# Attention units issued in a written order on every engine, with the identity and bias tables built on VectorE

## The chip, the core and the metric

The program runs on one core of a Trainium2 chip. The metric is the device time of one execution in microseconds (us). The kernel before took 1388.05 us, the median of three runs from 1387.29 to 1388.94.

## What is computed

Three layers, each fed by the one before. The sizes: 2 batches, 8 heads, 768 positions, 64 elements a head; then 1536 tokens of 512 elements, 8 experts of 512 to 1024 to 512.

```python
def _attn_ref(q, k, v, n_global, n_local):
    scores = scale * np.matmul(q, k.transpose(0, 1, 3, 2))
    rel = pos[:, None] - pos[None, :]
    is_global = pos[None, :] < int(n_global)
    is_local = (rel >= 0) & (rel < int(n_local))
    keep = is_global | is_local
    dist = np.where(is_global & ~is_local, float(n_local), np.abs(rel))
    scores = scores - slopes[:, None, None] * dist[None, :, :]
    scores = np.where(keep, scores, -1000000000.0)
    a = np.exp(scores - np.max(scores, axis=-1, keepdims=True))
    a = a / (np.sum(a, axis=-1, keepdims=True) + 1e-09)
    return np.matmul(a, v)

def _moe_ref(x, w_gate, w1, w2):
    P = np.exp(x @ w_gate - (x @ w_gate).max())
    for _ in range(8):
        P /= P.sum(1, keepdims=True) + 1e-09
        P /= P.sum(0, keepdims=True) + 1e-09
        P *= N / E
    for e in range(E):
        h = np.maximum(x @ w1[e], 0.0)
        out += P[:, e:e + 1] * (h @ w2[e])
    return out
```

The third layer has the same sizes with gate and weights of its own. Each token goes to one expert there, in the order of falling logits, up to 192 tokens an expert. With 8 global keys and 96 local ones, a query of the attention sees few keys.

## The kernel before

Products are made in three parts of 16 bits: a high half and the rest of each operand, high by high, high by low and low by high (`mm3`, lines 664 to 666). A matrix is first read for its largest magnitude (the tile wam, line 607 on VectorE), brought to a power of two, and split: high half on ScalarE (line 618), low half on VectorE (line 619).

The attention goes through 12 blocks of 128 queries, each in two **units** of four heads: 24 units t = 0 to 23, block t // 2. A block sees 232 keys (128 of its own, 96 before them, 8 global ones), the first block of each batch (units 0, 1, 12 and 13) only 128. The steps of a unit are functions of `band_attention`:

- `start`: q and k of a block are turned by TensorE through the identity (tiles pq and pk, lines 440 and 445), q copied by ScalarE (442) and k by VectorE (slab, 447). GpSimd adds the 104 other keys to the slab (450 to 453).
- `weigh`: TensorE makes the scores (ps, 465); VectorE adds the bias table of a head and takes the extreme (one custom instruction for a head, 471, here called the **softening**); ScalarE takes the exponential (474); VectorE makes the reciprocal of the sum (476, 477) and GpSimd multiplies by it (481, the **normalisation**).
- `turn`: TensorE turns the weights (pe, 491), ScalarE and VectorE copy them out (et, 496 and 494).
- `mix`: TensorE multiplies them with v (pa, 510).
- `split_x`: a finished block is split into halves (xt, 519 on ScalarE, 520 on VectorE), and multiplied with the gate (pg, lines 138 and 139; small instructions 142 and 145).

From unit 12 on, each unit also takes one of the 16 **early products** of expert 0 (ph, through `hidden`): 12 matmuls of 128x512, evacuated twice by ScalarE (657, 658) and once by VectorE (659). Fifteen of them are issued inside the loop over units. The weights of expert 0 are loaded, measured and split meanwhile by two generators, `early`, a step or two a unit.

The bias tables (`table`) and the identity come from ramps that GpSimd writes (jp, line 87; rel, lines 389 and 392). The narrow table's eight products are VectorE's, the wide one's GpSimd's:

```python
            eng = nc.vector if own_only else nc.gpsimd
            for h in range(H):
                eng.tensor_scalar(tb[:, h, :], rel, 2.0 ** (-8.0 * (h + 1) / H), NEG, op0=ALU.mult, op1=ALU.min)
```

The order in which an engine issues is set by a scheduler from the program's data dependences and its own estimates; the loop over units sets priorities only. Loads go through SP's queue in the order that it chose for SP.

Of the kernel before, what the change touches and what calls it, by code (L numbers as in the profile page):

```python
# [40 lines left out]
def tile_sparse_attention_moe_moe(ctx, tc, q, k, v, ng, nl, wg1, w11, w12, wg2, w21, w22, out, taps=None):  # L41
# [117 lines left out]
    gw1 = load_gate(wg1, "wg1")  # L159

    def attention(atp, aps):

        qtz = []
# [186 lines left out]
    def band_attention(atp, aps):  # L350


        order = [(b, i) for b in range(B) for i in range(NBLK)]
        NB = len(order)
        HU = HP // 2
# [14 lines left out]
        def load(n):  # L370
            if n >= NB:
                return
            qbs[n] = rows(q, n, "qb", 3)
            kbs[n] = rows(k, n, "kb", 3)
            b, i = order[n]
            if i:
# [7 lines left out]
        def table(own_only):  # L384
# [4 lines left out]
            nc.gpsimd.iota(rel[:, 0:P], pattern=[[-1, P]], base=0, channel_multiplier=1,  # L389
                           allow_small_or_imprecise_dtypes=True)  # L390
            if not own_only:
                nc.gpsimd.iota(rel[:, P:wl], pattern=[[-1, NP]], base=NP, channel_multiplier=1,
                               allow_small_or_imprecise_dtypes=True)
            m = atp.tile([P, W], F32, name=f"keep{W}")
# [14 lines left out]
            tabs.append(tb)  # L409

        scales, vams = {}, {}

        def magnitude(n):

            b, i = order[n]
            if i == 0:
                vams[b] = sml.tile([P, NBLK + 1], F32, name="vam")
            nc.vector.tensor_reduce(vams[b][:, i:i + 1], vos[n], axis=AX.XY, op=ALU.max, apply_absolute_value=True)

        def batch_scale(b):  # L420

            am = vams.pop(b)
            nc.vector.tensor_reduce(am[:, NBLK:], am[:, :NBLK], axis=AX.X, op=ALU.max)
            s = pow2_scale(am[:, NBLK:], "sv", bufs=2)
            f = sml.tile([P, 1], F32, name="gf")
            nc.vector.tensor_mul(f, s[:, 1:2], gw1[1][:, 1:2])
# [3 lines left out]
        slabs, kgs = {}, {}  # L430

        def start(n):

            b, i = order[n]
            S = SimpleNamespace(n=n, b=b, i=i, W=WB if i else P, nch=2 if i else 1, ex={}, et={}, pa=None)
            S.cks = [P, NP + ng][:S.nch]
            qb, kb = qbs.pop(n), kbs.pop(n)
            pt = aps.tile([P, HP, P], F32, name="pq", tag="tr", bufs=2)
            for p in range(HP):
                nc.tensor.transpose(pt[:, p, :], qb[:, 2 * p:2 * p + 2, :].rearrange("p h d -> p (h d)"), ident)  # L440
            S.qt = atp.tile([P, HP, P], F32, name="qt", bufs=2)
            nc.scalar.activation(S.qt, pt, AF.Copy, scale=qs)
            pt = aps.tile([P, HP, P], F32, name="pk", tag="tr", bufs=2)
            for p in range(HP):
                nc.tensor.transpose(pt[:, p, :], kb[:, 2 * p:2 * p + 2, :].rearrange("p h d -> p (h d)"), ident)
            S.slab = slabs[n] = atp.tile([P, HP, WB], F32, name="slab", bufs=3)
            nc.vector.tensor_copy(S.slab[:, :, 0:P], pt)
# [3 lines left out]
            else:  # L451
                nc.gpsimd.tensor_copy(S.slab[:, :, P:P + NP], slabs.pop(n - 1)[:, :, P - NP:P])
                nc.gpsimd.tensor_copy(S.slab[:, :, P + NP:], kgs[b])
            S.vs = [vos[n]] + ([vps.pop(n)] if i else [])
            return S

        def weigh(S, u):

            W = S.W
            ex = S.ex[u] = atp.tile([P, 2, 2, WB], F32, name="ex", bufs=3)  # L460
            st = sml.tile([P, 4, 4], F32, name="st4", bufs=4)
            ps = [aps.tile([P, 2, 256], F32, name=f"ps{j}", tag=f"sc{j}", bufs=1) for j in range(2)]
# [5 lines left out]
            for y in range(HU):  # L468
                for j in range(2):
                    z = 2 * y + j  # L470
# [57 lines left out]
        for n in range(1, NBLK + 1):  # L528
            load_own(n)
# [6 lines left out]
        for t in range(len(units) + 3):  # L536
            n, u = divmod(t, 2)
            if u == 0:
                load(n + 2)
                if n:  # L540
                    load_own(n + NBLK)
# [637 lines left out]
```

## Time and profile before

| | |
|---|---|
| median of the runs | 1388.05 us |
| the profiled execution | 1384.17 us |
| its span in the trace | 1382.3 us |
| TensorE busy | 1308.7 us, 95% of the span |
| VectorE busy | 808.3 us, 58% |
| ScalarE busy | 591.8 us, 43% |
| GpSimd busy | 211.3 us, 15% |
| attention, up to the end of the 15th early product | 171.1 us |

In the rows below PE is TensorE's matmuls, PEld its weight loads (they lie beside PE), DVE is VectorE, ACT is ScalarE, POOL is GpSimd. L471 is line 471 of the kernel. A row of a timeline gives the start in us, the duration in us, engine, line, operation, the tile written and the tile read, shape and count; in brackets the idle time of the engine before it and what ended that. Rows of the same kind that follow each other on an engine are drawn together, with their count.

### The profile page before, as it was taken

The numbers are of one execution on the slowest core, as the hardware profiler recorded it, in microseconds if no ns is written. First come the engines' busy times: TensorE is split into PE (matmuls) and PEld (weight loads), VectorE is DVE, ScalarE is ACT, GpSimd is POOL, SyncE is SP. The second block draws the span as 40 slices with busy tenths as digits, with TensorE's granted clock in tenths as the row PEclk, the third lists the DMA queues.
The fourth block names the chain that finished last, engine by engine and source line by source line (L and its number), as shares of the span: only waits on it lengthen the run. The fifth ranks groups of instructions, "written<-read, shape, count | busy, mean of one in ns | idle before, by whom it ended". The sixth has DMA issues, their size and how long they took to land.

```text
span 1382.3 us, 19944 instructions
## 1 busy us (share of the span) xinstructions
PE 1308.7 (95%) x7956; PEld 670.7 (49%) x7956; DVE 808.3 (58%) x1765; ACT 591.8 (43%) x1053; POOL 211.3 (15%) x323
## 2 busy tenths in 40 slices
PE   5899999999999999999899999999999989879998
PEld 3665544444444444444344444445545434337775
DVE  5777686554666466556546655575635898822121
ACT  3667551343243324333522434166553566613332
POOL 5233211010001000000100010000001333430100
PEclk8999999999999999999999999999999999989999
DMA  8352024151545135324424441431001111378640
GB/s 217 82 150 74 1 74 170 61 197 47 173 145 170 61 126 179 122 87 158 149 95 142 143 160 57 169 123 62 2 1 63 62 62 62 122 208 302 273 201 24
DMA packets 88557, 164.93 MB, mean 119 GB/s; under 512 B 50065, under 2 KB 50065, under 8 KB 85905
## 3 DMA queue, kind: packets, MB, share of 16 engines
q1 hardware_dynamic: 77040, 119.62, 26.7%
q0 software_dynamic: 11424, 44.05, 8.3%
q8 instruction: 62, 1.02, 0.3%
q14 instruction: 31, 0.25, 0.1%
HBM read 119.61 MB, written 44.05 MB: 118 GB/s over the span
## 4 chain that ended last, share of the span: by engine, by line
PE 47%; DVE 15%; issue 15%; DMA 13%; ACT 5%; POOL 5%; POOLq 0%; DVEq 0%; ACTq 0%
DMA raw<-in_moe_w_dram 7%; PE ph L664 7%; PE ph L666 7%; PE ph L665 7%; PE py L664 6%; PE py L665 6%; PE py L666 6%; DMA ws<-spill 6%; DVE wam L607 4%; DVE wslot L619 2%; POOL acc L761 2%; PE pe L491 2%; PE pa L510 2%; DVE xt L953 1%; DVE xt L955 1%
## 5 line engine op out<-in xcount | busy, mean ns | idle before, releaser
L664 PE MATMUL py<-wslot,hslot 128*128 128x512 f16 x768 | 291.3, 379 | 9.9 <-ACT relu L658 9.9
L664 PE MATMUL ph<-xt,wslot 128*128 128x512 f16 x768 | 291.4, 379 | 7.4 <-ACT relu L658 3.9
L665 PE MATMUL py<-wslot,hslot 128*128 128x512 f16 x768 | 291.3, 379 | 0.0
L666 PE MATMUL py<-wslot,hslot 128*128 128x512 f16 x768 | 291.3, 379 | 0.0
L666 PE MATMUL ph<-xt,wslot 128*128 128x512 f16 x768 | 291.3, 379 | 0.0
L665 PE MATMUL ph<-xt,wslot 128*128 128x512 f16 x768 | 291.2, 379 | 0.0
L657 ACT ACTIVATE hslot<-ph 128x512 f16<-128x512 f32 x192 | 114.5, 596 | 208.9 <-PE ph L666 208.7
L659 DVE TENSOR_TENSOR hslot<-relu,hslot 128x512 f16<-128x512 f32 x192 | 131.5, 688 | 119.6 <-ACT relu L658 118.6
L607 DVE TENSOR_REDUCE wam<-raw 128x1 f32<-128x1024 f32 (+1 forms) x136 | 152.5, 1149 | 74.6 <-DMA raw<-in_moe_w_dram 74.5
L618 ACT ACTIVATE spill<-raw,s 128x1024 f16<-128x1024 f32 x64 | 72.8, 1146 | 246.4 <-DVE s L114 129.8
L619 DVE SCALAR_TENSOR_TENSOR spill<-raw,s,spill 128x1024 f16<-128x1024 f32 x64 | 81.7, 1284 | 114.4 <-ACT spill L618 113.2
L658 ACT ACTIVATE relu<-ph 128x512 f32<-128x512 f32 (+1 forms) x224 | 130.1, 581 | 0.0
L665 PEld LDWEIGHTS <-hslot 128*128 128x128 f16 x768 | 75.3, 98 | 98.9 <-issue 13.6
L665 PEld LDWEIGHTS <-wslot 128*128 128x128 f16 x768 | 75.1, 98 | 93.8 <-issue 9.5
L664 PEld LDWEIGHTS <-hslot 128*128 128x128 f16 x768 | 75.3, 98 | 88.6 <-issue 2.5
L666 PEld LDWEIGHTS <-hslot 128*128 128x128 f16 x768 | 75.1, 98 | 88.5 <-issue 2.5
L666 PEld LDWEIGHTS <-wslot 128*128 128x128 f16 x768 | 75.1, 98 | 87.4
L664 PEld LDWEIGHTS <-wslot 128*128 128x128 f16 x768 | 75.1, 98 | 87.4 <-issue 2.4
L618 ACT ACTIVATE wslot<-raw,s 128x1024 f16<-128x1024 f32 (+1 forms) x72 | 70.9, 1047 | 72.3 <-PE py L666 48.7
L619 DVE SCALAR_TENSOR_TENSOR wslot<-raw,s,wslot 128x1024 f16<-128x1024 f32 (+1 forms) x72 | 81.2, 1159 | 4.3 <-ACT wslot L618 4.3
L650 POOL DMA_DIRECT2D ws<-spill x64 | 44.2, 692 | 220.8 <-DVE spill L619 220.5
L102 POOL PARTITION_ALL_REDUCE amax<-wam x30 | 10.6, 354 | 413.9 <-DVE wam L608 406.0
(245 smaller groups left out, 1652.6 us busy)
## 6 DMA issues: line engine op xcount, KB each, us to landing
raw<-in_moe_w_dram SPq DMA_DIRECT2D x64, 1024.0 KB, 5.9
ws<-spill POOLq DMA_DIRECT2D x64, 512.0 KB, 6.6
w2slot<-ws SPq DMA_DIRECT2D x16, 2048.0 KB, 10.2
hd<-hslot POOLq DMA_DIRECT2D x2, 2048.0 KB, 7.2
hslot<-hd SPq DMA_DIRECT2D x2, 2048.0 KB
qb<-in_q_dram SPq DMA_DIRECT2D x12, 256.0 KB, 3.4
kb<-in_k_dram SPq DMA_DIRECT2D x12, 256.0 KB, 6.6
vo<-in_v_dram SPq DMA_DIRECT2D x12, 256.0 KB, 3.7
```

What stands on the lines that cost most here:

```text
L491: nc.tensor.transpose(pe[:ck, y, j, :], ex[:, y, j, a * P:a * P + ck], ident)
L510: nc.tensor.matmul(S.pa[64 * j:64 * j + 64, p, :], S.vs[a][:ck, 2 * p + j, :], ets[a][:ck, y, j, :], start=a == 0, stop=a == S.nch - 1, ti ...
L607: nc.vector.tensor_reduce(am[:, y:y + 1], raw, axis=AX.X, op=ALU.max, apply_absolute_value=True)
L618: nc.scalar.activation(hi, raw, AF.Copy, scale=s[:, 0:1])
L619: nc.vector.scalar_tensor_tensor(lo, raw, s[:, 0:1], hi, op0=ALU.mult, op1=ALU.subtract)
L650: nc.gpsimd.dma_start(dr[:, :, a * q4:a * q4 + q4], t)
L657: nc.scalar.activation(hi, ps, AF.Relu, scale=HS)
L658: nc.scalar.activation(r[:, :n], ps, AF.Relu, scale=HS)
L659: nc.vector.tensor_sub(lo, r[:, :n], hi)
L664: nc.tensor.matmul(out_, lhs(0, a), rhs(0, a), start=a == 0, stop=False)
L665: nc.tensor.matmul(out_, lhs(0, a), rhs(1, a), start=False, stop=False)
L666: nc.tensor.matmul(out_, lhs(1, a), rhs(0, a), start=False, stop=a == n - 1)
```

## The change

1. The ramp `colx` is written on VectorE by doubling, turned in squares of 32 to a column `rowx`, and identity, jp and both tables come from these two. GpSimd writes no ramp, and the wide table's eight products are VectorE's.
2. The attention's trace of instructions is fixed in its written order on every engine, SP included, through dependences without a semaphore (`in_order`).
3. The loop over units is written anew for that order: scores, the next block's turned q and k (odd units), mixing of unit t−2, turning of unit t−1, the gate product (even units), the early product. The early product's evacuation stands ahead of the next unit's softenings. The first one follows unit 13 in place of unit 12.
4. The weights of expert 0 (`matrix`) are split into eight parts each: two magnitudes a unit, then two splits a unit; every second low half is a multiplication and a subtraction on GpSimd.
5. ScalarE and VectorE change places in the copies of the turned weights; the gate's weights are scaled in steps inside the loop; loads are issued in another order.

The core of the difference:

```diff
-    jp = cst.tile([P, P], I32)
-    nc.gpsimd.iota(jp, pattern=[[1, P]], base=0, channel_multiplier=-1)
+    colx = cst.tile([P, P], F32)
+    nc.vector.memset(colx[:, 0:1], 0.0)
+    n = 1
+    while n < P:
+        nc.vector.tensor_scalar(colx[:, n:2 * n], colx[:, 0:n], float(n), None, op0=ALU.add)
+        n *= 2
+    jp = cst.tile([P, P], F32)
+    blk = jp[:, 0:32]
+    nc.vector.transpose(blk, colx[:, 0:32])
+    rowx = cst.tile([P, 1], F32)
+    for g in range(P // 32):
+        nc.vector.tensor_scalar(rowx[32 * g:32 * g + 32], blk[32 * g:32 * g + 32, 0:1], 32.0 * g, None, op0=ALU.add)
     ident = cst.tile([P, P], F32)
-    nc.vector.tensor_scalar(ident, jp, 0.0, None, op0=ALU.is_equal)
+    nc.vector.tensor_scalar(ident, colx, rowx, None, op0=ALU.is_equal)
...
+    @contextmanager
+    def in_order():
+        traced = nc.cur_bb.bb.instructions
+        last = traced[-1]
+        yield
+        start = next(k for k in reversed(range(len(traced))) if traced[k] is last) + 1
+        before = {}
+        for i in traced[start:]:
+            if i.engine in before:
+                tc.add_manual_dep(i, before[i.engine].name,
+                                  mybir.DependencyInfo(mybir.DependencyClass.NoSync, mybir.DependencyReason.DATA),
+                                  reason="in_order")
+            before[i.engine] = i
...
-            eng = nc.vector if own_only else nc.gpsimd
             for h in range(H):
-                eng.tensor_scalar(tb[:, h, :], rel, 2.0 ** (-8.0 * (h + 1) / H), NEG, op0=ALU.mult, op1=ALU.min)
+                nc.vector.tensor_scalar(tb[:, h, :], rel, 2.0 ** (-8.0 * (h + 1) / H), NEG, op0=ALU.mult, op1=ALU.min)
...
+                nc.scalar.activation(hi, part, AF.Copy, scale=s[:, 0:1])
+                if a % 2:
+                    nc.gpsimd.tensor_scalar(part, part, s[:, 0:1], 0.0, op0=ALU.mult, op1=ALU.add)
+                    nc.gpsimd.tensor_tensor(lo, part, hi, op=ALU.subtract)
+                else:
+                    nc.vector.scalar_tensor_tensor(lo, part, s[:, 0:1], hi, op0=ALU.mult, op1=ALU.subtract)
...
-        for t in range(len(units) + 3):
+        for t in range(NU + 4):
             n, u = divmod(t, 2)
...
+            if t == 1:
+                next(weights)
+            if S:
+                scores(S, u)
+            block = None
+            if u and n + 1 < NB:
+                block = turn_block(n + 1)
+                next(block)
+            if 0 <= t - 2 < NU:
+                m, x = divmod(t - 2, 2)
+                mix(blocks[m], x)
...
+                last = turn(blocks[m], x)
+                next(last)
+            if evac is not None:
+                finish(evac)
+                evac = None
+            for z in range(4):
+                if S:
+                    soften(S, u, z)
+                if z == 0 and block:
+                    next(block)
+            if block:
+                finish(block)
...
+            for x in running:
+                next(x)
+                next(x)
+            if t == 0:
+                table(False)
...
+            for i in magnitudes.get(t, ()):
+                magnitude(i)
+            if S:
+                normalise(S, u)
+            if last:
+                finish(last)
+            for x in running:
+                finish(x)
+            running = []
...
+            elif t >= 4:
+                for _ in range(2):
+                    if not owing:
+                        owing = next(weights, None) == "bank"
+            if mixed and mixed[0].b in scales:
+                x = split_x(mixed.pop(0))
+                next(x)
+                running.append(x)
+            if first_hidden and (0, 0) in W and all(c in split for c in range(first_hidden[0][1] * CPB,
...
+                evac = first_products(*first_hidden.pop(0))
+                next(evac)
...
-            band_attention(atp, aps)
+            with in_order():
+                band_attention(atp, aps)
```

The listings of the two kernels' orders show what moves. **GpSimd at the start**, before (jp and rel are the ramps, kg the global keys, tab_211 the wide table, ex the weights that are normalised; the ISA of line 87 is the library switch for the ramps):

```order
L87 ISA
L87 IOTA jp 128x128
L389 IOTA rel_154 128x128
L389 IOTA rel_201 128x128
L392 IOTA rel_201 128x96
L450 COPY kg<-slab 128x32
L452 COPY slab<-slab 128x4x96
L453 COPY slab<-kg 128x4x8 x2
L452 COPY slab<-slab 128x4x96
L408 TENSOR_SCALAR tab_211<-rel_201 128x232 x2
L481 TENSOR_SCALAR ex<-ex,st_180 128x128 x4
L408 TENSOR_SCALAR tab_211<-rel_201 128x232 x6
```

and now:

```order
L549 COPY kg<-slab 128x32
L583 ISA
L583 TENSOR_SCALAR ex<-ex,st_187 128x128 x4
L541 COPY slab<-slab 128x4x96
L542 COPY slab<-kg 128x4x8
L583 TENSOR_SCALAR ex<-ex,st_255 128x128 x4
```

The ramps and the wide table have left GpSimd, and its library switch stands behind the copy of the global keys, ahead of the first normalisation.

**TensorE in an even unit with an early product**, before (the end of a product, then the gate product pg):

```order
L666 LDWEIGHTS wslot
L666 MATMUL ph<-xt,wslot 128x512
L138 LDWEIGHTS xt
L138 MATMUL pg<-wg1hl,xt 128x16
L139 LDWEIGHTS xt
L139 MATMUL pg<-wg1hl,xt 128x16
```

and now:

```order
L632 LDWEIGHTS xt
L632 MATMUL pg<-wg1hl,xt 128x16
L634 LDWEIGHTS xt
L634 MATMUL pg<-wg1hl,xt 128x16
L839 LDWEIGHTS wslot
L839 MATMUL ph<-xt,wslot 128x512
```

The gate product has moved from behind the unit's early product to in front of it.

**VectorE in the same unit**, before (from the last softening of a unit to the first of the next):

```order
L471 ISA ex,st_1205<-ps_1207,tab_211 128x232
L471 ISA st_1205 128x1
L607 TENSOR_REDUCE wam_946<-raw 128x1
L608 TENSOR_REDUCE wam_946<-wam_946 128x1
L494 COPY et<-pe 104x512
L476 TENSOR_SCALAR st_1205<-st_1205 128x4
L477 RECIPROCAL st_1205<-st_1205 128x4
L520 SCALAR_TENSOR_TENSOR xt<-pa,sv,xt 128x4x128
L142 TENSOR_SCALAR gt<-pg,gf 128x8
L659 TENSOR_TENSOR hslot<-relu,hslot 128x512
L145 SCALAR_TENSOR_TENSOR logits<-pg,gf,gt 128x8
L471 ISA ex,st_1285<-ps_1286,tab_211 128x232
```

and now:

```order
L569 ISA ex,st_1296<-ps_1265,tab_206 128x232
L569 ISA st_1296 128x1
L626 SCALAR_TENSOR_TENSOR xt<-pa,sv,xt 128x4x128
L578 TENSOR_SCALAR st_1296<-st_1296 128x4
L579 RECIPROCAL st_1296<-st_1296 128x4
L602 COPY et<-pe 128x512
L638 TENSOR_SCALAR gt<-pg,gf 128x8
L639 SCALAR_TENSOR_TENSOR logits<-pg,gf,gt 128x8
L500 TENSOR_REDUCE wam_1080<-raw 128x1 x2
L834 TENSOR_TENSOR hslot<-relu,hslot 128x512
L569 ISA ex,st_1386<-ps_1341,tab_206 128x232
```

The low half of x (xt) stands directly behind the four softenings, which stand behind the subtraction of the early product before.

## Rows read from the trace of the kernel before

**Rows 1.** Windows: stretch, its us, busy PE, PEld, DVE, ACT, POOL, granted clock, DMA share, GB/s.
```profile
0.00:13.00 13.00, 4.22 (x23) 3.47 (x24) 5.80 (x33) 2.68 (x4) 2.22 (x10) 1.00 0.88 196
13.00:83.00 70.00, 57.45 (x430) 39.91 (x430) 51.90 (x199) 42.25 (x131) 33.41 (x71) 0.85 0.53 132
50.00:58.00 8.00, 7.55 (x34) 5.12 (x32) 5.41 (x22) 4.64 (x13) 3.67 (x9) 0.58 0.01 3
83.00:171.00 88.00, 85.79 (x650) 51.24 (x647) 63.21 (x214) 54.97 (x152) 26.96 (x59) 1.00 0.25 72
171.00:280.00 109.00, 109.00 (x507) 49.47 (x506) 76.67 (x161) 38.42 (x55) 11.52 (x20) 1.00 0.30 103
```

**Rows 2.** Timeline of TensorE at the end of the attention.
```profile
168.55 0.38 PE L664 MATMUL ph<-xt,wslot 128*128 128x512 f16 x1
...
171.14 0.27 PE L105 MATMUL bc<-ident,gam 128*128 128x128 f32 x1
```

**Rows 3.** Timeline of the start, all engines.
```profile
6.80 0.69 DVE L418 TENSOR_REDUCE vam<-vo 128x1 f32<-128x512 f32 x1 [3.98 <-DMA vo<-in_v_dram]
...
8.10 0.23 POOL L87 IOTA jp<- 128x128 int32 x1 [7.66 <-issue]
...
8.94 1.06 PE L440 MATMUL pq<-ident,qb 128*128 128x128 f32 x4
...
11.77 1.17 DVE L408 TENSOR_SCALAR tab<-rel 128x128 f32<-128x128 f32 x8
...
12.88 0.29 DVE L471 CUSTOM_DVE_ANT_0 ex<-ps,tab 128x128 f32<-128x128 f32 x1
...
17.57 1.42 POOL L481 TENSOR_SCALAR ex<-ex,st 128x128 f32<-128x128 f32 x4
...
19.08 6.31 POOL L408 TENSOR_SCALAR tab<-rel 128x232 f32<-128x232 f32 x6
...
19.45 1.93 PE L465 MATMUL ps<-slab,qt 64*128 64x232 f32 x8
```

**Rows 4.** What lines 87 and 707 issued: count, ns, first and last start.
```profile
L87 POOLq MODIFY_POOL_CONFIG  x2: 11/11/11, 0.8 to 0.8; - x2
...
L707 POOLq MODIFY_POOL_CONFIG  x2: 11/11/11, 166.4 to 166.5; - x2
L707 POOL PARTITION_ALL_REDUCE gm<-gm x1: 377/377/377, 172.1 to 172.1; - x1
```

**Rows 5.** Timeline of one even unit with an early product.
```profile
141.73 1.05 PE L465 MATMUL ps<-slab,qt 64*128 64x232 f32 x8
...
142.33 0.59 ACT L658 ACTIVATE relu<-ph 128x512 f32<-128x512 f32 x1
...
142.96 0.69 DVE L659 TENSOR_TENSOR hslot<-relu,hslot 128x512 f16<-128x512 f32 x1 [0.27 <-ACT relu L658]
...
143.57 0.39 DVE L471 CUSTOM_DVE_ANT_0 ex<-ps,tab 128x232 f32<-128x232 f32 x1
...
144.78 0.39 PE L664 MATMUL ph<-xt,wslot 128*128 128x512 f16 x1
...
144.85 0.69 DVE L494 COPY et<-pe 104x512 f32<-104x512 f32 x1
```

**Rows 6.** First softenings of units 4 and 12, and the first early product.
```profile
35.16 0.40 DVE L471 CUSTOM_DVE_ANT_0 ex<-ps,tab 128x232 f32<-128x232 f32 x1 [0.19 <-PE ps L465]
...
80.98 0.28 DVE L471 CUSTOM_DVE_ANT_0 ex<-ps,tab 128x128 f32<-128x128 f32 x1
...
83.43 0.39 PE L664 MATMUL ph<-xt,wslot 128*128 128x512 f16 x1
```

**Rows 7.** Groups by form up to 172 us: busy us, mean ns | idle before.
```profile
L619 DVE SCALAR_TENSOR_TENSOR wslot<-raw,s,wslot 128x512 f16<-128x512 f32 x16 | 11.7, 742 | 0.0
```

**Rows 8.** Timeline of GpSimd late in the program, two instructions with two inputs each.
```profile
1196.85 5.75 POOL L761 TENSOR_TENSOR acc<-acc,relu 128x512 f32<-128x512 f32 x1 [5.43 <-ACT relu L760]
1204.01 1.09 POOL L761 TENSOR_TENSOR acc<-acc,relu 128x512 f32<-128x512 f32 x1 [1.41 <-ACT relu L760]
```

More of the change, by code (lines that the diff above doesn't have):

```diff
@@ L368, in load_own, with load_qk, load_past @@
                 vos[n] = rows(v, n, "vo", 8)
[L370 to L376, printed above, removed]
+        def load_qk(n):
+            if n < NB:
+                qbs[n] = rows(q, n, "qb", 3)
+                kbs[n] = rows(k, n, "kb", 3)
+        def load_past(n):
+            if n < NB and order[n][1]:
+                b, i = order[n]
                 t = atp.tile([P, H, D], F32, name="vp", bufs=3)
@@ L434, in start, with matrices, turn_block @@
+        def matrices():
+            for which in range(2):
+                yield from matrix(which)
+        slabs, kgs, blocks = {}, {}, {}
+        def turn_block(n):
             b, i = order[n]
-            S = SimpleNamespace(n=n, b=b, i=i, W=WB if i else P, nch=2 if i else 1, ex={}, et={}, pa=None)
+            S = blocks[n] = SimpleNamespace(n=n, b=b, i=i, W=WB if i else P, nch=2 if i else 1, ex={}, et={}, pa=None,
+                                            st={}, ps={})
             S.cks = [P, NP + ng][:S.nch]
@@ L531, in band_attention @@
         nc.scalar.activation(warm, ones[:, 0:1], AF.Exp)
-        blocks = {0: start(0)}
         table(True)
-        units = [(n, u) for n in range(NB) for u in range(2)]
-        splits = []
-        for t in range(len(units) + 3):
+        finish(turn_block(0))
+        weights = matrices()
+        running = []
+        owing = False
+        evac = None
+        magnitudes = {0: (0,), 1: (1, 2), 2: (3, 4), 3: (5,)}
+        magnitudes.update({t: (t - 3,) for t in range(9, 9 + NBLK)})
+        mixed = []
@@ L537, in band_attention @@
+        scaling = None
+        for t in range(NU + 4):
             n, u = divmod(t, 2)
+            S = blocks.get(n) if t < NU else None
             if u == 0:
[L539 to L547 removed]
@@ L548, in band_attention @@
-            for x in splits:
-                next(x, None)
-            if t < len(units):
-                weigh(blocks[n], u)
+                load_qk(n + 3)
+                load_past(n + 1) if n else None
+                load_own(n + 6)
+            if t == 1:
[9 more added lines that the diff above has]
+                mix(blocks[m], x)
+                if x:
+                    mixed.append(blocks.pop(m))
@@ L552, in band_attention @@
+            if owing:
+                next(weights)
+                owing = False
+            for x in running:
+                next(x)
+                next(x)
             if t == 0:
                 table(False)
[L554 to L563 removed]
@@ L586, in tile_sparse_attention_moe_moe @@
+        for x in running:
+            finish(x)
+        finish(weights)
     pools = {}
@@ L734, in tile_sparse_attention_moe_moe @@
         pools["h", n] = lat
-    for x in first_hidden:
-        hidden(*x)
+    for e, tb, f in first_hidden:
+        hidden(e, tb, [f])
     hidden(0, NTB - 1)
```

235 lines of the change are left out of this document (149 added, 86 removed).

## The prediction

> **What bounds the kernel now.** I read the table of windows first, then the timeline of the start, the timelines of one unit in the middle and of the end of the attention, and last the groups by form.
>
> The windows [rows 1] say which stage a gain can come from. From 171 to 280 us TensorE is busy 109 of 109 us. Its order there is the same in both kernels, so whatever makes the attention end earlier is passed on one for one. The profiled execution took 1384.17 us, 3.9 below the median of 1388.05. I work the sum out as a difference and take it from the median. One part in 500, 2.8 us, is about what a measurement of this kernel can tell from no change.
>
> The attention ends when the 15th early product of expert 0 ends: it starts at 168.55 and the next work stands at 171.14 [rows 2]. Twelve matmuls take 2.59 us.
>
> The start [rows 3]: GpSimd's first own instruction, the ramp jp, comes at 8.10, and behind it the identity, the four transposes of q at 8.94, and the first softening of scores at 12.88. The third load on SP, v of block 0, had landed by 6.80, and q and k stand ahead of it. Thus not the data but GpSimd was late. Why: the line of jp issues a library switch at 0.8 and runs at 8.1, and another switch at 166.4 is followed by its first work at 172.1 [rows 4]. A switch costs 5.7 to 7.3 us.
>
> Between 13 and 83 us TensorE is busy 57 of 70 us, VectorE 52, so hand-overs bind; from 83 to 171 TensorE has 86 of 88 [rows 1].
>
> **The change, part by part.** Times are starts of the first softening of a unit, before and now.
>
> *Start.* The identity now needs some 13 short VectorE instructions. From the 128-wide table's eight products, 1.17 us together [rows 3], 0.15 each, and a transpose of 0.2 to 0.7, they end near 3.7. q and k then bind: below the 6.80 of the load behind them, I take 4.5. Two groups of transposes at 1.06 each [rows 3], a copy of k at 0.69 and scores at 1.0 (sizes of the copy at 144.85 and the scores at 141.73, [rows 5]): first softening at 8.3 instead of 12.88, **4.6 earlier**. Ends: 7.5 if q and k are there with the identity, 10.6 if only with v.
>
> *Units 0 to 3.* GpSimd's library switch isn't gone. It stands in front of the first normalisation now, behind the copy of the global keys at 8.4. At 5.7 to 7.3 us [rows 4], unit 0 is normalised from 14.1 to 15.7 on instead of 17.57. The wide table's eight products leave GpSimd, where six of them took 6.31 us ahead of unit 1's normalisation. On VectorE I price them at 0.27 each, the narrow product scaled by 232/128: 2.1 us, beside the library switch. What is late next is TensorE, which has idled: eight score matmuls took 1.93 us at 19.45 [rows 3] against 1.05 at 141.73 [rows 5]. I put unit 4's softening at 31.0 against 35.16 [rows 6], **4.2 earlier**. Ends: 1.9 earlier, if only the smaller library gain is kept; 6.3 more, 8.2 earlier, if the six products' time is saved whole.
>
> *Units 4 to 12.* Before, 35.16 to 80.98 [rows 6], 5.73 a unit. Now VectorE's written order has per unit: four softenings 1.28 and a copy of the turned weights 0.69 [rows 5], two short ones 0.35; an odd unit the copy of k 0.69, an even one the low half of x 0.74 and two small ones 0.45; and either two magnitudes of W1, 0.69 each as for v in [rows 3], or one low half at 0.74 [rows 7] with the other on GpSimd. That is 4.6 in the mean, with 0.4 of waits 5.05; eight units and 1.1 for W1's scale give 41.5, so unit 12 starts at 72.5 against 80.98, **8.5 earlier**. Ends: 4.7 and 5.73 a unit, 69.7 and 76.8.
>
> *First product.* It stood in unit 12 and now ends unit 13, so one more unit lies ahead of it. With 3.7 us each for units 12 and 13 (128 keys) it starts at 80.0 against 83.43 [rows 6].
>
> *Units with a product.* From an odd unit on, TensorE's order is scores, eight transposes, sixteen mixing matmuls, product: the first three take 3.05 us from 141.73 to the product at 144.78 [rows 5]. An even unit's new order puts the gate product of x ahead of the product, and it waits for VectorE. From the product's end at 141.73: two evacuations on ScalarE end at 142.92, the subtraction leads to softenings at 143.57, the fourth ends at 144.85 [rows 5], that is 3.1 us behind; the low half of x 0.74, the gate product 0.25 and the product 2.59 make 6.7. Without that wait the unit would be 3.05 + 0.2 + 2.59 = 5.8. An odd unit has the transposes of q and k, 1.06 each at the low pace [rows 3], 1.15 both at the ratio 1.05 to 1.93: 3.05 + 1.15 + 2.59 = 6.8, with a hand-over of 0.2 7.0. Nine units, 14 to 22, five even: 61.5. Then the last five products (12.9) with units 22 and 23 turned and mixed (6.8): 19.7. The first product itself takes 2.6. So the 15th ends at 80.0 + 2.6 + 61.5 + 19.7 = 163.8 against 171.14: **7.3 us earlier**.
>
> Edits without a cost of their own: W2's splits in units 19 to 22 lie beside products of 2.59. W1's two loads of 1 MB now stand behind some 4 MB on SP, read by VectorE at the end of unit 4, near 34; at the 196 GB/s of the first 13 us [rows 1] the first half lands near 27, the second at 32. Were they late, every softening behind them on VectorE would be too.
>
> The time is 1388.05 − 7.3 = 1380.8, say **1381**.
>
> *A rule against the change.* On GpSimd an instruction with two inputs took 5.75 us at 1196.85 and 1.09 at 1204.01 [rows 8]; the change gives GpSimd four such subtractions on W1 and four on W2. I take 1.1, since each has a unit's time to end in. The Trainium skill ("SBUF — State Buffer", section "SBUF: two separate sides") says that VectorE and GpSimd share a port pair under an exclusive lock, taken by a VectorE instruction with two SBUF inputs, which blocks the other for its whole length. By it the subtractions would stretch, and the sum go towards the last rival; that VectorE's softenings read PSUM on one side speaks against much of it.
>
> **Rivals.**
>
> *The waits go too (0.18).* If the low half of x is ready early, even units take TensorE's own 5.8 and odd ones 6.8: 56.2 for nine instead of 61.5, and 4.7 a unit in units 4 to 12 takes another 2.8: 1388.05 − 7.3 − 5.3 (− 2.8), 1373 to 1375. For it: TensorE has 86 of 88 us in that stretch now [rows 1]. Against: the written order leaves it no other work to put in the gap.
>
> *The order eats the gain (0.16).* If a written order costs one hand-over more in each unit, of the size of the 0.27 that VectorE waits for ScalarE at 142.96 [rows 5], 20 units lose 5.4 us: 1386. For it: VectorE, ScalarE and TensorE each now wait for the other in every unit. Against: the earlier start isn't touched by it.
>
> *The clock falls (0.11).* From 50 to 58 us TensorE was granted 0.58 of full speed, which lies near the lower of its levels, 1.2 of 2.4 GHz, and before 0.85 in the mean of 13 to 83; from 83 on it was 1.00 [rows 1]. If units 4 to 12 ran at the lower level, 3.75 us of TensorE's work a unit (3.05, and half of the 1.15 and 0.25 that odd and even ones add) would take 6.9 by the ratio 1.93 to 1.05, 1.85 more than 5.05; nine units are 17 us: 1388.05 − 7.3 + 17 = 1398, slower. It decides from six such units on. For it: VectorE alone sets the pace there and TensorE has gaps. Against: before, with gaps as large, most of the stretch had the full level.
>
> *GpSimd blocked (0.05).* At 5.75 instead of 1.09 each, GpSimd's subtractions take 4.7 us more. The normalisation stands behind them on the same queue, and TensorE's transposes wait for it. Four for W1, and half of W2's, hidden partly: 19 to 28 us, 1400 to 1409. For it, [rows 8]; against, the shorter of the two durations there is of the next such instruction on the same queue.
>
> That the change doesn't do what it says can be left out for the order itself, as the listing of the order shows it; that it starts late, from q and k at 6.5, is inside the range.
>
> **How the numbers follow.** The forecast has 0.50; its own range is 1378 to 1385, from the ends of unit 12's start, 2.8 before and 4.3 behind the value taken. Faster by over 0.2% (below 1385.3): the forecast and the first rival, 0.68. Within 0.2%: the second rival, 0.16. Slower (over 1390.8): the last two, 0.16. The range, 8 in 10, goes from 1369 to 1392: it takes in the first rival with the fuller start, the forecast, the second rival, and a clock that falls for a unit or two.
>
> **What would show it.** First softening near 8.3 and unit 4's near 31. GpSimd's switch between its copy at 8.4 and a normalisation near 15. First product near 80, even units of 6.7 with TensorE waiting for the low half of x ahead of the gate product; the 15th product's end at 163.8, and a shift of 7 us from there to the end that stays constant. Wrong would make it: unit 4 no earlier than 33, a granted clock below 0.8 over units 4 to 12, GpSimd subtractions over 3 us, or a shift that shrinks behind 171.

## The result: slower by half a per cent, and where the time went

The changed kernel is slower. Of 15 runs each, its median is 1392.38 us and that of the kernel before 1386.09 us; the ratio is 1.0055, with an interval of 1.0042 to 1.0068. By the ratio that is 7.6 us more (the two medians differ by 6.3) where 7.3 us less was forecast. The profiled execution took 1392.16 us (span 1390.4).

The start came out as forecast. The timeline of the changed kernel, and what line 583 issued (count, ns, first and last start):

```profile
4.34 1.08 PE L534 MATMUL pq<-ident,qb 128*128 128x128 f32 x4 [4.34 <-DVE rel L424]
...
7.33 0.21 POOL L549 COPY kg<-slab 128x32 f32<-128x32 f32 x1 [6.89 <-DVE slab L546]
...
8.64 0.29 DVE L569 CUSTOM_DVE_ANT_0 ex<-ps,tab 128x128 f32<-128x128 f32 x1 [1.37 <-PE ps L557]
...
15.29 1.41 POOL L583 TENSOR_SCALAR ex<-ex,st 128x128 f32<-128x128 f32 x4 [7.75 <-DVE st L569]
...
30.82 0.40 DVE L569 CUSTOM_DVE_ANT_0 ex<-ps,tab 128x232 f32<-128x232 f32 x1 [1.50 <-PE ps L557]
...
71.90 0.28 DVE L569 CUSTOM_DVE_ANT_0 ex<-ps,tab 128x128 f32<-128x128 f32 x1
...
78.35 0.38 PE L839 MATMUL ph<-xt,wslot 128*128 128x512 f16 x1
```

```profile
L583 POOLq MODIFY_POOL_CONFIG  x2: 11/11/11, 7.6 to 7.6; - x2
```

These answer to [rows 3], [rows 4] and [rows 6]: first softening 8.64 instead of 12.88, unit 4 at 30.82 instead of 35.16, unit 12 at 71.90 instead of 80.98, first early product at 78.35 instead of 83.43. GpSimd's library switch is issued at 7.6, and the first normalisation runs at 15.29. Up to here the change has won 5 us and has one more unit behind it.

All of it, and more, is lost while the early products run. Unit 14 of the changed kernel, TensorE and VectorE:

```profile
81.03 1.05 PE L557 MATMUL ps<-slab,qt 64*128 64x232 f32 x8
...
82.87 0.39 DVE L569 CUSTOM_DVE_ANT_0 ex<-ps,tab 128x232 f32<-128x232 f32 x1
...
84.14 0.75 DVE L626 SCALAR_TENSOR_TENSOR xt<-pa,sv,xt 128x512 f16<-128x512 f32 x1
...
84.95 0.18 PE L634 MATMUL pg<-wg1hl,xt 128*128 128x16 f16 x1 [1.68 <-DVE xt L626]
...
86.66 0.15 DVE L478 TENSOR_REDUCE vam<-vam 128x1 f32<-128x6 f32 x1
...
86.96 0.45 PE L440 MATMUL bc<-ident,vam 128*128 128x128 f32 x1 [1.68 <-DVE vam L478]
...
87.19 0.63 PE L839 MATMUL ph<-xt,wslot 128*128 128x512 f16 x1
...
92.29 1.05 PE L557 MATMUL ps<-slab,qt 64*128 64x232 f32 x8
```

TensorE stands twice in front of a product that needs nothing of what it waits for: 1.68 us for the low half of x, which the gate product reads, and 1.68 us for the magnitude of the second batch's v, whose scale is spread by a transpose (bc). Then the product itself is slow: from 87.19 to the next scores at 92.29 are 5.1 us, where the same twelve matmuls took 2.59 [rows 2]. Each matmul has 0.63 us in place of 0.38. The windows (columns as in [rows 1]) say why:

```profile
84.00:92.00 8.00, 5.38 (x20) 2.11 (x20) 2.74 (x10) 1.30 (x6) 2.36 (x6) 0.58 0.55 85
119.00:123.00 4.00, 3.22 (x9) 1.37 (x10) 0.60 (x2) 0.00 (x0) 1.42 (x4) 0.57 0.00 0
173.00:177.20 4.20, 3.18 (x15) 1.26 (x16) 2.58 (x10) 0.37 (x1) 0.38 (x1) 0.62 0.00 0
185.00:280.00 95.00, 95.00 (x442) 43.08 (x441) 62.92 (x118) 30.63 (x44) 7.22 (x13) 1.00 0.33 111
```

In three stretches among the products the granted clock is near 0.6, that is mostly at the lower of the two levels, 1.2 of 2.4 GHz. Before, it was 1.00 in the whole of 83 to 171 [rows 1]. Ahead of each of the three TensorE had stood for 2 to 3.4 us, in one or two pieces with a few short matmuls between. Not every stand is followed by a slow product: behind 1.88 us ahead of 150.80 and behind 2.56 us ahead of 164.59 the granted clock stayed at 1.00. From 185 us on TensorE is busy without a gap, as before.

The end of the attention, where VectorE is late again:

```profile
160.93 2.34 DVE L784 TENSOR_REDUCE wam<-raw 128x1 f32<-128x1024 f32 x2 [1.18 <-DMA raw<-in_moe_w_dram]
...
163.79 0.74 DVE L626 SCALAR_TENSOR_TENSOR xt<-pa,sv,xt 128x512 f16<-128x512 f32 x1
...
164.59 0.18 PE L634 MATMUL pg<-wg1hl,xt 128*128 128x16 f16 x1 [2.56 <-DVE xt L626]
...
174.02 0.20 PE L634 MATMUL pg<-wg1hl,xt 128*128 128x16 f16 x1 [2.11 <-DVE xt L626]
...
180.96 0.27 PE L116 MATMUL bc<-ident,gam 128*128 128x128 f32 x1
```

The last row answers to the second of [rows 2]: the 15th product ends at 180.96 instead of 171.14, 9.8 us later. The next expert's magnitudes (L784), which don't belong to the attention's written order, have come in front of the low half of x.

The start of each evacuation of a product (the relu on ScalarE) shows how the shift grows and what stays of it. In us against the kernel before, negative is earlier; e stands for the runs below:

| evacuation | before at | changed | e1 | e2 | e3 | e6 | e8 | e10 | e11 | e15 |
|---|---|---|---|---|---|---|---|---|---|---|
| 1st | 87.3 | −5.7 | −5.7 | −5.8 | −6.3 | −6.9 | −9.6 | −11.4 | −7.9 | −4.5 |
| 6th | 118.7 | +6.0 | −5.6 | −2.7 | −7.0 | −6.7 | −9.6 | −10.4 | −2.9 | +5.4 |
| 11th | 154.0 | +6.2 | −5.2 | −2.4 | −6.3 | −8.3 | −13.4 | −9.6 | −3.0 | +5.0 |
| 15th | 171.8 | +9.8 | −3.0 | +1.2 | −10.0 | −10.9 | −17.1 | −8.7 | −6.6 | +5.1 |
| 25th | 260.5 | +9.4 | −3.4 | +0.7 | −10.0 | −3.0 | −17.1 | −9.1 | −6.6 | +5.1 |
| 191st | 1045.5 | +7.4 | −6.4 | −2.9 | −12.9 | −4.9 | −19.0 | −12.2 | −8.5 | +3.5 |

(The changed kernel's and all others' first evacuation belongs to a product that stands behind one more unit than before's, except where the order is free. A column comes from one profiled execution; that of e6 took 1380.39 us, 3.6 less than the median of its runs.)

### The profile page after: what moved, and what is told of

It reads as the page before. It is cut to its first block, busy times and chain, and to the rows that moved or that the text cites. A ratio compares the mean times of both kernels' runs of the same rounds, so it can differ in the third digit from the quotient of the medians.

```text
span 1390.4 us, 19993 instructions
## 1 busy us (share of the span) xinstructions
PE 1303.0 (94%) x7956; PEld 667.7 (48%) x7956; DVE 811.9 (58%) x1786; ACT 587.5 (42%) x1049; POOL 214.7 (15%) x327
## 4 chain that ended last, share of the span: by engine, by line
PE 46%; DVE 17%; issue 14%; DMA 12%; ACT 6%; POOL 4%; POOLq 0%; DVEq 0%; ACTq 0%
PE py L840 7%; PE py L841 7%; PE py L839 7%; DMA raw<-in_moe_w_dram 7%; PE ph L839 7%; PE ph L841 7%; PE ph L840 7%; DMA ws<-spill 5%; DVE wam L784 3%; POOL acc L937 2%; ACT ex L572 1%; DVE wslot L796 1%; DVE xt L1129 1%; DVE xt L1131 1%; DVE hslot L834 1%
## 5 line engine op out<-in xcount | busy, mean ns | idle before, releaser
L784 DVE TENSOR_REDUCE wam<-raw 128x1 f32<-128x1024 f32 x120 | 142.5, 1213 | 78.8 <-DMA raw<-in_moe_w_dram 78.6
L840 PEld LDWEIGHTS <-hslot 128*128 128x128 f16 x768 | 75.4, 98 | 100.1 <-issue 15.2
L795 ACT ACTIVATE wslot<-raw,s 128x1024 f16<-128x1024 f32 x56 | 60.5, 1143 | 77.3 <-PE py L841 62.4
L796 DVE SCALAR_TENSOR_TENSOR wslot<-raw,s,wslot 128x1024 f16<-128x1024 f32 x56 | 69.5, 1278 | 4.0 <-ACT wslot L795 4.0
```

Of the source, the lines that this page charges most:

```text
L784: nc.vector.tensor_reduce(am[:, y:y + 1], raw, axis=AX.X, op=ALU.max, apply_absolute_value=True)
L795: nc.scalar.activation(hi, raw, AF.Copy, scale=s[:, 0:1])
L796: nc.vector.scalar_tensor_tensor(lo, raw, s[:, 0:1], hi, op0=ALU.mult, op1=ALU.subtract)
L840: nc.tensor.matmul(out_, lhs(0, a), rhs(1, a), start=False, stop=False)
```

## The experiments

The theory after reading the two traces (A): TensorE's written order puts work that waits for VectorE ahead of a product that could run, TensorE stands, and its clock falls. Rivals: (B) any written order costs hand-overs; (C) GpSimd's halves of the splits block VectorE; (D) the next expert's work stands in VectorE's way. All ratios are against the kernel before on the same chip, with their intervals; "less than the changed kernel" is the difference of the two ratios times 1386 us.

### e1: the product first

```diff
+            if first_hidden and (0, 0) in W and all(...):
+                evac = first_products(*first_hidden.pop(0))
+                next(evac)
             for z in range(4):
                 if S:
                     soften(S, u, z)
```

(moved up from the unit's end; W of expert 0 is published one step earlier)

> The changed kernel with each early product put directly behind the turning of unit t-1, ahead of the gate product and of the scales' transposes (and the first matrix published one step earlier, so that the first product stays in unit 13). Theory A (TensorE stands still ahead of the product, for the low half of x and for the two scales, and its clock falls behind the longest stands): the waits on L626 and on the scale inside units 13 to 27 (about 10 and 4 us) and the three stretches at a granted clock near 0.6 (about 5 us) go; even units near 5.9 us, odd ones near 6.9; 15 to 19 us less than the changed kernel, 1373 to 1378. Theory B (a written order costs hand-overs wherever they stand): no more than 3 us less, 1389 or more. Theory C (GpSimd's halves of the splits block VectorE): a few us less, 1385 to 1389, with units 20 to 23 as slow as now.

Measured: 1380.55 us, ratio 0.9973 (0.9960 to 0.9986), 11.4 us less than the changed kernel and 0.3% faster than before. TensorE in unit 14:

```profile
81.00 1.05 PE L558 MATMUL ps<-slab,qt 64*128 64x232 f32 x8
...
86.93 0.29 PE L440 MATMUL bc<-ident,vam 128*128 128x128 f32 x1 [0.92 <-DVE vam L478]
87.15 1.05 PE L558 MATMUL ps<-slab,qt 64*128 64x232 f32 x8
```

6.15 us for the unit instead of 11.26; the same gate product and the same transpose now wait beside or behind the product. B's bound (no more than 3 us) has fallen. The size is 4 us short of A's 15 to 19. The table has 13 us won at the 15th evacuation; from the 11th to the 15th e1 itself loses 2.2 us against before, where the next expert's magnitudes stand in front of the low half of x on VectorE (from 151.89) and TensorE stands 2.35 us (ahead of 155.56; e6 below).

### e2: only the scales' transposes behind the product

> The changed kernel with the product ahead of the scales' transposes only; the gate product stays ahead of it. Theory A: units 14 and 18 lose their waits of 1.7 and 2.3 us for the scale and their stretches at the low clock (2.5 and 1.4 us), 6 to 8 us less than the changed kernel, 1384 to 1386; units 20 to 27 keep their waits for the low half of x. Theories B and C: within 2 us of the changed kernel.

Edit: the same block, put ahead of the lines that start `scaling` and the step of `weights`, behind the gate product. Measured: 1384.45 us, ratio 1.0005 (0.9993 to 1.0018), 6.9 us less than the changed kernel, as A had it. The window from 83 to 100 covers the units where the changed kernel's clock fell first:

```profile
83.00:100.00 17.00, 13.82 (x113) 8.54 (x112) 12.74 (x52) 10.19 (x32) 4.47 (x11) 1.00 0.54 102
```

With one stand of 1.68 us left instead of two, the clock stays at 1.00 there. Units 14 and 18 now take 6.89 us each instead of 11.26 and 10.88. So the two scales are worth 6.9 us, most of what the change loses against before.

### e3: no written order

```diff
-            with in_order():
-                band_attention(atp, aps)
+            band_attention(atp, aps)
```

> The changed kernel without in_order: the same instructions, the scheduler chooses. Theory A and B: the early start stays (first softening near 8.6) and the stands ahead of the products are filled with other work, 1378 to 1382. Theory C: the halves on GpSimd still cost, 1386 or more.

Measured: 1371.57 us, ratio 0.9906 (0.9887 to 0.9926): 20.7 us less than the changed kernel and 13 less than before, more than either theory had forecast (1378 to 1382). The same instructions in the scheduler's order keep the start's gain, place products in the stands and take no loss in the last units (15th evacuation 10.0 earlier).

### e10 and e11: whose order is it?

```diff
         for i in traced[start:]:
+            if i.engine == mybir.EngineType.PE:    # e10; in e11 !=
+                continue
```

> The changed kernel with the written order on every engine but TensorE. Theory A (the loss is TensorE's own order: gate product and scales ahead of the product): TensorE fills the stands, 10 to 15 us less than the changed kernel, 1377 to 1382, as with the product first. If the order of VectorE, ScalarE and GpSimd costs as much by itself: 1386 or more.

> The changed kernel with the written order on TensorE alone. Theory A: TensorE still stands ahead of its products, though VectorE may make the low half of x earlier: 1384 to 1390. Theory D and B (the order of the other engines): most of the loss is gone, 1378 or less.

Measured: TensorE free, the others in order 1375.25 us, ratio 0.9936 (0.9919 to 0.9953), 16.5 us less than the changed kernel, a little more than A's 10 to 15. TensorE alone in order 1378.19 us, ratio 0.9958 (0.9941 to 0.9975), 13.4 less. The second is a miss of theory A as I had put it: TensorE's order is the changed kernel's, with the gate product ahead, and does little harm. The reason is in its trace, where a free VectorE makes the low half of x a unit early (77.22), so that the gate product starts at 80.90 without a wait; what is left there is the stand in front of the scale's transpose (the row names the last VectorE instruction that was waited for, not the magnitude itself). Behind this single stand of 1.92 us seven matmuls of the product ran at the slow pace, and unit 14 took 8.81 us, against 11.26 in the changed kernel and 6.15 in e1:

```profile
77.22 0.72 DVE L628 SCALAR_TENSOR_TENSOR xt<-pa,sv,xt 128x512 f16<-128x512 f32 x1
...
80.90 0.17 PE L634 MATMUL pg<-wg1hl,xt 128*128 128x16 f16 x1
...
83.17 0.44 PE L442 MATMUL bc<-ident,vam 128*128 128x128 f32 x1 [1.92 <-DVE logits L641]
```

Narrowed, A says that neither order alone makes the loss: it takes TensorE's place for the reader (gate product, scale) and VectorE's place for the writer (the low half behind four softenings) together.

### e12, e15 and e13: the writer moved, the order kept

```diff
             for x in running:
-                next(x)
                 next(x)
...
                 x = split_x(mixed.pop(0))
                 next(x)
+                next(x)
```

> The changed kernel, order kept on every engine, with one VectorE instruction of a block moved: the low half of x at the end of the odd unit instead of behind the next unit's four softenings. TensorE's order is untouched, gate product ahead of the product. Theory A, as narrowed (each order by itself is harmless; together TensorE's place for the gate product and VectorE's place for the low half make a stand in every even unit): the waits on the low half, 0.8 to 2.6 us in seven units, go; those for the two scales and the clock behind them stay; 7 to 11 us less than the changed kernel, 1381 to 1385. If the order as a whole costs: within 3 us of the changed kernel, 1389 or more.

Measured: 1391.36 us, ratio 1.0046 (1.0034 to 1.0058), only 1.2 less: a miss in the total. The trace (of an execution of 1396.12 us, 4.8 above the median) parts it: from the first evacuation to the 15th it takes 92.5 us instead of 100.1, the forecast gain, but unit 12 starts at 77.86 instead of 71.90. In units 5, 6 and 8 VectorE waits 0.98 to 1.11 us for ScalarE's exponentials instead of 0.32 to 0.44, since the low half no longer stands in front of that wait; for ScalarE's high half it waits only in units 9 and 11, 0.44 and 0.32 us. The largest step, 2.6 us in unit 9, comes from TensorE: behind unit 8 it stands 3.39 us for W1's scale at 56.62 instead of 1.62, and from 56 to 62 the granted clock is 0.51 instead of 0.84. So I moved the instruction from unit 13 on only:

> As the run with the low half early, but only from unit 13 on, so that units 0 to 12 are the changed kernel's own. If the even units' stands come from VectorE's place for the low half (theory A, narrowed), the stretch from the first evacuation to the 15th falls from 100.1 us to near 92.5, as it did in the run that moved all of them, and this time the total shows it: first softenings up to unit 13 within 0.5 us of the changed kernel, 6 to 9 us less than the changed kernel, 1383 to 1386. If the moved instruction only shifts the stand to another place in those units: within 3 us of the changed kernel.

Measured: 1386.32 us, ratio 1.0014 (0.9999 to 1.0028), 5.7 less than the changed kernel, a little short of the 6 to 9. Unit 16 takes 5.83 us instead of 6.79, and the stretch from the first evacuation to the 15th 94.1 instead of 100.1. In units 14 and 18 little is won (10.34 and 10.90 us, against 11.26 and 10.88): the stand has only moved to the scale, which VectorE reaches no sooner. The condition on the start was not met: from unit 10 on the softenings come 1.2 us later than the changed kernel's, with a granted clock of 0.60 from 56 to 62 instead of 0.84. Why is open.

```profile
88.09 0.45 PE L440 MATMUL bc<-ident,vam 128*128 128x128 f32 x1 [3.45 <-DVE vam L478]
```

With both moves in order:

> Both moves in the written order: product ahead of gate product and scales, and the low half of x at the end of the odd unit. Theory A: little is left for the second, since the gate product then stands behind 2.6 us of products; 0 to 3 us less than product first alone, 1377 to 1381; what is left against the kernel without order is the last units, where VectorE waits for the next expert's load.

Measured: 1380.31 us, ratio 0.9967 (0.9953 to 0.9980), the same as e1 within the intervals. Units 14 to 21 take the same as e1's to 0.1 us: once the product stands first, the low half's place matters no more there. Its cost in units 5 to 13 (first evacuation 0.7 earlier than before, e1 5.7) is made good from the 11th evacuation to the 15th, where e13 gains 3.5 us against before and e1 loses 2.2.

### e6: the next expert's work kept behind the attention

```diff
+    for i in traced[end:]:
+        if i.engine == mybir.EngineType.DVE:
+            tc.add_manual_dep(i, tail[i.engine].name, ...)
```

> The run with the product first, and every VectorE instruction that the program issues behind the attention also kept behind it, so that the next expert's magnitudes can't stand ahead of the attention's last evacuations. Theory D (in a written order VectorE waits for the next expert's load, 1.8 and 3.6 us idle and 2.35 us of work each, in front of the subtraction on which the rest of the attention hangs): the 15th product ends near 163 instead of 167.7, 4 to 6 us less than product first, near 1375. Theory B (other hand-overs of the order): within 1.5 us of product first, 1379 to 1382, or slower where the next expert's scale then comes late.

Measured: 1384.00 us, ratio 1.0002 (0.9991 to 1.0013), 4 us more than e1: a miss, but an instructive one. The attention does end earlier, as D had it: the 15th evacuation is 10.9 us ahead of before's, where e1 has 3.0 and e3, without an order, 10.0. Then 8 us go again before the 25th, in one stand of TensorE and in the product behind it (granted clock 0.71 from 211 to 216):

```profile
210.73 0.58 PE L843 MATMUL py<-wslot,hslot 128*128 128x512 f16 x1 [6.27 <-DVE acc L943]
```

The magnitudes moved behind the attention fill VectorE (37.6 of 44 us from 160 to 204) just where the balancing of the gate runs, and the weighting of the first output waits for that. The work was in the attention's way, but it has to be done by then. The profiled execution shows where the 8 us go; it is as long as e1's (1380.38), and the 4 us that the median has more are not in it.

### e4, e8 and e16: GpSimd's halves

```diff
-                if a % 2:
-                    nc.gpsimd.tensor_scalar(part, part, s[:, 0:1], 0.0, op0=ALU.mult, op1=ALU.add)
-                    nc.gpsimd.tensor_tensor(lo, part, hi, op=ALU.subtract)
-                else:
-                    nc.vector.scalar_tensor_tensor(...)
+                nc.vector.scalar_tensor_tensor(...)
```

> The changed kernel with every low half of expert 0's weights on VectorE, none on GpSimd (eight instructions of 0.74 us more on VectorE, sixteen fewer on GpSimd). Theory C (GpSimd's subtractions and VectorE's block each other): the subtractions of units 20 and 23 fall back from 1.52 to 0.69 us, GpSimd's normalisations from 2.19 to 1.76; 2 to 4 us less than the changed kernel, 1388 to 1390. Theory A: VectorE is what TensorE waits for, so the added work costs, 0 to 5 us more, 1392 to 1397.

> No written order and every low half of expert 0's weights on VectorE. Theory C (the halves on GpSimd cost by blocking VectorE): 2 to 4 us less than the run without order. Theory A: they are hidden either way, within 2 us, or up to 4 more since VectorE gets 6 us more work.

> Written order, product first, and every low half on VectorE. If GpSimd's halves cost through VectorE wherever TensorE no longer stands for something else, as in the kernels without order (7 us): 3 to 8 us less than product first, 1372 to 1378. If in a written order VectorE's added 6 us bind in units 9 to 12 and cost what the halves give back: within 2 us of product first, 1379 to 1383.

Measured: on the changed kernel (e4) 1393.27 us, ratio 1.0059 (1.0039 to 1.0079), nothing won in total, so C alone doesn't explain the loss. Its trace shows part of C: all 15 subtractions of the products' evacuations on VectorE up to 185 us took 0.63 to 0.69 us again, where the changed kernel has two of 1.52, unit 21 takes 7.06 us instead of 7.89, and from the 11th evacuation to the 15th 3.5 us less are lost. Against it, VectorE's added work makes the first evacuation 2.6 us later, and four normalisations took up to 2.63 us beside its low halves, not 1.76. On the kernel without order (e8) **1365.47 us, ratio 0.9854** (0.9837 to 0.9872), 7.2 us less than e3, more than C's 2 to 4, and the fastest of all, 20 us under the kernel before. On e1 (e16) 1378.56 us, ratio 0.9953 (0.9936 to 0.9971), 2.8 less than e1, between the two expectations and within the intervals. In its trace both happen: units 10 to 12 take 0.8 us more each, and from the first evacuation to the 15th it takes 82.1 us, e1 87.2. What the halves cost in e3, where three of them stand together on GpSimd:

```profile
119.59 1.17 POOL L513 TENSOR_TENSOR wslot<-raw,wslot 128x512 f16<-128x512 f32 x1
...
121.96 1.16 POOL L513 TENSOR_TENSOR wslot<-raw,wslot 128x512 f16<-128x512 f32 x1
```

```profile
119.78 1.53 DVE L834 TENSOR_TENSOR hslot<-relu,hslot 128x512 f16<-128x512 f32 x1
...
122.19 1.48 DVE L515 SCALAR_TENSOR_TENSOR wslot<-raw,s,wslot 128x512 f16<-128x512 f32 x1
```

```profile
128.02 0.76 PE L594 MATMUL pe<-ident,ex 128*128 128x128 f32 x2 [0.90 <-POOL ex L583]
...
131.86 0.63 PE L839 MATMUL ph<-xt,wslot 128*128 128x512 f16 x1
```

VectorE's subtraction takes 1.53 us instead of 0.69 [rows 5] and its low half 1.48 instead of 0.74 [rows 7], each begun while GpSimd's two-input subtraction ran; the normalisation comes late, TensorE stands, and the product behind runs at 0.63 a matmul. By the table 4.5 of the 7 us between e3 and e8 arise here, between the 6th evacuation and the 11th; the other 2.6 are there before, from where is open.

### e5: the ramp alone

Edit: the kernel before with identity, ramps and both tables on VectorE (the two tables' masks share a buffer for it).

> The kernel before with only the ramp, identity and both tables moved to VectorE; order left to the scheduler. If the start's gain is passed on to the end: first softening near 9 instead of 12.9 and 3 to 6 us less than before, 1380 to 1383. If it is given back at a later wait (the scale of v at 27.8 us, the loads): within 1.5 us of before.

Measured: 1380.82 us, ratio 0.9981 (0.9966 to 0.9996), 2.6 us less than before, between the two expectations. First softening at 9.40; of these 3.5 us 1.3 are left at unit 4's softening (33.89 instead of 35.16) and 1.1 at the first evacuation. What takes the rest between units 2 and 4 is open; VectorE waits 1.96 us for the scores of unit 3.

### e14: no order, product first

> No written order, product written ahead of the gate product. Theory A: without an order the scheduler has filled the stands already; within 3 us of the run without order, 1369 to 1375.

Measured: 1372.72 us, ratio 0.9914 (0.9895 to 0.9934), as e3 (0.9906): without a written order the place in the program matters no more. Against e1, the same program in order, it is 8 us less; the first matmul of e14's first product stands at 67.53, ahead of unit 13's scores (69.65); e1's stands at 78.32, behind the whole of unit 13's.

Taken together: e1 wins back 11.4 of the 20.7 us that the written order costs against e3. By e6 the next expert's work on VectorE accounts for what e1 lacks against e3 at the 15th evacuation; whether a written order can have the early end without the later wait was not tested.

## Why the prediction was wrong

**Right, to a microsecond or two:** every term up to the first product. Start 8.3 (8.64), unit 4 at 31.0 (30.82), unit 12 at 72.5 (71.90), first product at 80.0 (78.35). The switch stands in front of the first normalisation at 15.29, inside 14.1 to 15.7. VectorE's transpose in the ramp, put at 0.2 to 0.7 from no row, took 0.20. Also right in the main was that the shift behind the attention stays: +9.8 at its end, +9.4 at the 25th evacuation, +7.4 at the 191st.

**Right by luck: the pace of 5.05 us.** The terms listed for a unit add up to 4.6 only where two magnitudes stand in it; with the one low half of the other four units they add up to 4.0, 4.3 in the mean. VectorE was busy 34.56 of the 41.08 us from unit 4 to unit 12, which is 4.3 a unit, and idle 0.8 a unit, where 0.4 and a share of the 1.1 for W1's scale were allowed. Too much work and too little waiting cancel.

**Wrong: "Nine units, 14 to 22, five even: 61.5".** The step that failed is a wait put at nothing: the transposes of two scales, which stand in front of products, and the lower clock behind them. The units took 72.6 us, from the scores at 81.03 to those at 153.67. The working of an ordinary unit holds: odd units 7.0 were 7.06 (15), 7.06 (17) and 7.05 (19), even ones 6.7 were 6.79 (16 and 20):

```profile
99.35 1.05 PE L557 MATMUL ps<-slab,qt 64*128 64x232 f32 x8
...
103.27 0.18 PE L634 MATMUL pg<-wg1hl,xt 128*128 128x16 f16 x1 [0.80 <-DVE xt L626]
...
106.14 1.05 PE L557 MATMUL ps<-slab,qt 64*128 64x232 f32 x8
```

What was missed is units 14 and 18, 11.26 and 10.88 us. In both a scale is spread by a transpose ahead of the product. I had priced that for W1 in units 4 to 12, at 1.1, and left the two others out: in unit 14 a second stand of 1.68, in unit 18 one of 2.34. Behind each the clock was down: 2.5 and 1.5 us more for the product. e2, which takes the two transposes out of the way, confirms it with 6.9 us. Units 21 and 22 add 2 us: 0.8 through GpSimd's halves in unit 21 (e4 has 7.06 there), and in unit 22 a wait of 1.88 for the low half of x, which the next expert's magnitudes hold up on VectorE (with them moved behind, e6 has 5.81 for this unit, e1 6.72).

**Wrong: the tail, "the last five products … 19.7".** It took 27.3 (153.67 to 180.96). I let the products run back to back; TensorE stood 0.53, 2.56 and 2.11 for xt and paid some 1.5 for the clock. The two misses of 11.1 and 7.6 us, less the 1.6 won before unit 14, are the 17 us between 163.8 and 180.96.

**The rivals.** The clock's fall was named, but for units 4 to 12 and at 17 us; there it stayed at 1.00 but for 50 to 60 (0.83). The mechanism decided elsewhere, in the products, where some stands are paid twice. "The order eats the gain" named one hand-over of 0.27 a unit; the loss sits in four units and the tail, and the order as a whole costs nearly four times that rival's 5.4 (20.7 us against e3). "The waits go too" is what e1 shows in part: units 16 and 20 take 5.81 us, the rival's 5.8, but units 17, 18 and 21 over 7.5. "GpSimd blocked" had the wrong victim: its subtractions took 1.16 to 1.70 us, not 5.75; it is mainly VectorE that is stretched:

```profile
132.36 0.69 DVE L834 TENSOR_TENSOR hslot<-relu,hslot 128x512 f16<-128x512 f32 x1 [1.49 <-ACT relu L833]
...
139.14 1.52 DVE L834 TENSOR_TENSOR hslot<-relu,hslot 128x512 f16<-128x512 f32 x1 [1.70 <-ACT relu L833]
```

```profile
132.37 1.70 POOL L513 TENSOR_TENSOR wslot<-raw,wslot 128x512 f16<-128x512 f32 x1
...
138.96 1.16 POOL L513 TENSOR_TENSOR wslot<-raw,wslot 128x512 f16<-128x512 f32 x1
```

The first pair starts within 0.01 us, VectorE ahead: VectorE takes its usual 0.69 and GpSimd 1.70 instead of 1.16. The second VectorE subtraction starts 0.18 behind GpSimd's and ends 0.54 behind its end. The Trainium skill ("SBUF — State Buffer", section "SBUF: two separate sides") has the port pair go to whichever starts first, for its whole instruction, with the other blocked; these rows agree with it in both directions, and in size but for 0.15 us: the one that starts second ends that much sooner than its usual time behind the other's end.

The chances were wrong in their weights as well: the argument that the written order "leaves it no other work to put in the gap" stood in the text as a word against the first rival, and was not carried into a price for the slower side.

## What to carry to other kernels

Where an order is written by hand, go through each engine's row and ask of every instruction that waits for another engine what stands behind it that could run; a small reader (a gate product, a scale's transpose) belongs behind the long work that doesn't need it. For the gate product moving its writer on the other engine did as well among the products (e15, units 16 and 20); for the scales only the reader's move was tried. Price every such instruction, the rare ones too: two transposes in 24 units made most of this loss. A stand of TensorE costs its own length, and in some places the lower clock on what follows; and work taken out of the way is only free if its own reader can wait.

## What was not expected of the hardware

A stand of some 3.4 us, broken by short matmuls, was followed by a product of 5.1 us in place of 2.6, so the clock cost nearly as much as the wait; with a stand of 1.68 alone (e2) the clock stayed at 1.00. The length of a stand doesn't decide it by itself: one of 1.92 us (e11, ahead of 83.17) was followed by seven slow matmuls, one of 2.56 (the changed kernel, ahead of 164.59) by none. What does is open here. VectorE's instructions with two inputs in SBUF took 1.5 us in place of 0.7 when begun 0.2 us behind GpSimd's two-input subtraction; with the subtractions gone (e4, e8) no such subtraction of VectorE took over 0.69. Neither was measured by itself.
